# The second product of the MLP as plain matrix products in all eight batches

## The chip, the cores and the metric

The kernel runs on one core of one Trainium2 chip. The metric is the device time of one execution in microseconds, as the median of several runs. TensorE is called PE here, VectorE DVE, ScalarE ACT, GpSimd POOL and SyncE SP. SP issues nearly all transfers.

## What is computed

The inputs are q, k, v (8 batches, 8 heads, 576 tokens, 64 features), p (32 packed tokens for each batch and head) and the MLP's `w_in` (512 x 2048), `w_out` (2048 x 512) and `beta` (2048).

```python
def sm_attn(qq, kk, vv):
    s = scale * np.matmul(qq, kk.transpose(0, 1, 3, 2))
    a = np.exp(s - np.max(s, axis=-1, keepdims=True))
    return np.matmul(a / (np.sum(a, axis=-1, keepdims=True) + 1e-09), vv)
p_packed = sm_attn(p, k, v)                 # 32 tokens for each head
out = sm_attn(q, p_packed, p_packed)        # 576 tokens for each head
x = out.transpose(0, 2, 1, 3).reshape(4608, 512)
h = x @ w_in
g = h * (1.0 / (1.0 + np.exp(-beta * h)))
result = g @ w_out                          # the second product
```

## The kernel before

The work is done batch by batch, 576 tokens each: 512 "main" tokens and 64 "rest" tokens. The attention's value product is folded into the MLP's first matrix: for each batch the packed values are multiplied by `w_in` (`fused_w`, steps `w`; eight matmuls on 32-column strips of the array), and the result, scaled by the softmax sum and by beta, is `W_bf` (steps `W`, DVE). The hidden layer is then `W_bf` times the attention weights `A2T`: 16 steps `h` for a batch, each two matmuls of 512 columns into one PSUM bank, followed by SiLU on ACT (steps `g`, line 827). The 64 rest tokens are done in two steps `hr` of 16 small matmuls and two steps `gr` on ACT; the rests of two batches share one tile.

The second product, `g @ w_out`, has two forms:

- Batches named in `PLAIN` (0 and 1) use `product` in `plan_mlp`: for each block `t` of 128 tokens, 16 matmuls of 512 columns are summed in one of two output banks (eight steps `o` of two matmuls). A `take` on DVE copies the bank to SBUF; batch 0 is taken in two halves (`HALVED`), the second by an `add`.
- Batches 2 to 7 use `plan_seven`: the product is cut into 2 x 2 blocks and computed with seven block products where the plain way needs eight. Each of `P1` to `P7` is 16 matmuls of 256 columns in four quarters (keys `p` and `P`). Sums and differences of blocks of `g` are made on DVE (`S` 1 to 4, line 1013), those of blocks of `w_out` once (`T4`, line 987). Ten reads (`R`, lines 1043 and 1045) for each such batch, shared by DVE and ACT, combine the partial results.

The rest tokens of each pair of batches have a plain block of their own, `t = 4`, in both forms.

Attention of a batch, in PE's steps: `s1r` and `s1` (scores of p and k), `z1` (sums), `pun` (packed values), `s2` (scores of q), `z2` (sums). Between them ACT does the exponentials (`e1`, `e2`, `l2`, `n2`; line 397 loads an activation table at each change between exponential and SiLU) and DVE makes `A2`. In batches 0 and 1, k and q are transposed on PE (`tr`); from batch 2 on by a DMA transpose that SP issues (line 527) when the casts to bf16 on POOL (line 463) are done. `p_tr` transposes p of batches 2 to 7, after its copy `p_dup` on POOL.

The order on each engine is written out by hand: `SEQUENCE` holds one list for each engine, and each engine works through its list in order, waiting at a step until what it needs is there. `Planner.run` only merges the lists into one program; the costs given to each task serve that merge, and they set how many filler matmuls on an identity matrix (`keep_warm`) are put into gaps that the merge sees on PE in the first 60 us. SP's list is also the order of transfers: inputs of batches 0 and 1 in pieces, four 1 MB pieces each of `w_in` and `w_out` through three staging buffers, then one batch after the other. The rests of a batch are two small transfers (`ld b x 2`, line 442).

Of the kernel before, what the change touches and what calls it, by code (L numbers as in the profile page):

```python
# [8 lines left out]
B, H, S, D = 8, 8, 576, 64  # L9
# [15 lines left out]
SR = 64  # L25
# [13 lines left out]
WN = 1  # L39
# [6 lines left out]
TILED_US = 0.095  # L46
PORT = ("S", "T4", "A2", "cast", "w_in", "w_out", "p_dup", "p0_bf")
PLAIN = (0, 1)
# [7 lines left out]
        ("brow", 0), ("tr", 0, "k", 0), ("tr", 0, "k", 1), ("p0_tr", 0), ("p0_tr", 1), ("bcol",), ("brow", 1),  # L56
        ("trr", 0, "k"), ("s1r", 0), ("tr", 0, "q", 0), ("brow", 2), ("s1", 0, 1), ("s1", 0, 0), ("tr", 0, "q", 1),
        ("z1", 0), ("pun", 0, 0), ("pun", 0), ("brow", 3), ("s2", 0, 0), ("z2", 0, 0), ("z2", 0, 1), ("w", 0, 0),
        ("w", 0, 1), ("h", 0, 1), ("h", 0, 2), ("tr", 1, "k", 0), ("h", 0, 0), ("h", 0, 3), ("tr", 1, "k", 1),
        ("o", 0, 0, 1), ("o", 0, 1, 1), ("h", 0, 7), ("h", 0, 4), ("o", 0, 1, 3), ("w", 0, 2), ("trr", 1, "k"),  # L60
        ("o", 0, 0, 3), ("h", 0, 5), ("h", 0, 8), ("s1r", 1), ("trr", 0, "q"), ("h", 0, 6), ("o", 0, 1, 5),
        ("s1", 1, 0), ("o", 0, 0, 5), ("o", 0, 0, 7), ("h", 0, 11), ("s1", 1, 1), ("h", 0, 9), ("o", 0, 1, 7),
        ("o", 0, 2, 1), ("w", 0, 3), ("o", 0, 2, 3), ("o", 0, 3, 1), ("o", 0, 3, 3), ("o", 0, 2, 5), ("z1", 1),
        ("o", 0, 3, 5), ("h", 0, 14), ("o", 0, 2, 7), ("h", 0, 15), ("tr", 1, "q", 0), ("h", 0, 13), ("pun", 1, 0),
        ("h", 0, 12), ("pun", 1), ("tr", 1, "q", 1), ("h", 0, 10), ("o", 0, 3, 7), ("s2", 0, 1), ("s2", 1, 0),
        ("o", 0, 1, 9), ("o", 0, 0, 9), ("w", 1, 0), ("o", 0, 0, 11), ("o", 0, 1, 11), ("z2", 1, 0), ("o", 0, 1, 13),
        ("trr", 1, "q"), ("o", 0, 1, 15), ("z2", 1, 1), ("z2", 0, 2), ("o", 0, 0, 13), ("o", 0, 0, 15),
        ("o", 0, 3, 9), ("o", 0, 3, 11), ("s2", 1, 1), ("w", 1, 1), ("o", 0, 2, 9), ("o", 0, 3, 13), ("z2", 1, 2),
        ("o", 0, 2, 11), ("w", 1, 2), ("o", 0, 2, 13), ("h", 1, 2), ("o", 0, 2, 15), ("h", 1, 1), ("o", 0, 3, 15),
        ("h", 1, 0), ("w", 1, 3), ("h", 1, 5), ("h", 1, 3), ("p_tr", 1), ("h", 1, 4), ("o", 1, 0, 1), ("h", 1, 11),  # L70
        ("p_tr", 0), ("h", 1, 6), ("o", 1, 0, 3), ("h", 1, 8), ("o", 1, 1, 1), ("h", 1, 9), ("h", 1, 10),
        ("o", 1, 1, 3), ("hr", 0, 0), ("h", 1, 7), ("o", 1, 0, 5), ("o", 1, 1, 5), ("s1r", 2), ("hr", 0, 1),
        ("s1", 2, 1), ("o", 1, 0, 7), ("s1", 2, 0), ("h", 1, 15), ("o", 1, 0, 9), ("o", 1, 0, 11), ("o", 1, 1, 7),
        ("z1", 2), ("pun", 2, 0), ("o", 1, 1, 9), ("pun", 2), ("o", 1, 1, 11), ("h", 1, 13), ("h", 1, 12),
        ("w", 2, 0), ("w", 2, 1), ("h", 1, 14), ("o", 1, 1, 13), ("hr", 1, 0), ("o", 1, 0, 13), ("o", 1, 0, 15),
        ("hr", 1, 1), ("o", 1, 1, 15), ("s2", 2, 0), ("w", 2, 2), ("o", 1, 2, 1), ("o", 1, 2, 3), ("z2", 2, 0),
        ("o", 1, 2, 5), ("z2", 2, 1), ("o", 1, 3, 1), ("s2", 2, 1), ("o", 1, 2, 7), ("o", 1, 2, 9), ("o", 1, 3, 3),
        ("o", 1, 2, 11), ("o", 1, 2, 13), ("o", 1, 2, 15), ("o", 1, 3, 5), ("o", 1, 3, 7), ("z2", 2, 2), ("h", 2, 0),
        ("h", 2, 6), ("o", 1, 3, 9), ("s1r", 3), ("o", 1, 3, 11), ("h", 2, 1), ("s1", 3, 1), ("o", 1, 4, 1),
        ("o", 1, 3, 13), ("s1", 3, 0), ("o", 1, 4, 3), ("w", 2, 3), ("o", 1, 4, 5), ("o", 1, 4, 7), ("h", 2, 2),  # L80
        ("o", 1, 4, 9), ("o", 1, 3, 15), ("z1", 3), ("pun", 3, 0), ("h", 2, 7), ("h", 2, 3), ("pun", 3),
        ("o", 1, 4, 11), ("h", 2, 8), ("h", 2, 11), ("w", 3, 0), ("w", 3, 1), ("h", 2, 9), ("h", 2, 10),
        ("o", 1, 4, 13), ("o", 1, 4, 15), ("h", 2, 5), ("h", 2, 13), ("w", 3, 2), ("w", 3, 3), ("h", 2, 4),
        ("h", 2, 12), ("p", 2, 1, 0), ("p", 2, 1, 1), ("h", 2, 15), ("h", 2, 14), ("p", 2, 1, 2), ("P", 2, 1),
        ("hr", 2, 0), ("p", 2, 2, 0), ("hr", 2, 1), ("p", 2, 2, 1), ("p", 2, 2, 2), ("s2", 3, 0), ("s2", 3, 1),
        ("P", 2, 2), ("p", 2, 6, 0), ("p", 2, 6, 1), ("z2", 3, 0), ("p", 2, 6, 2), ("P", 2, 6), ("z2", 3, 1),
        ("z2", 3, 2), ("p", 2, 5, 0), ("p", 2, 5, 1), ("s1r", 4), ("s1", 4, 1), ("p", 2, 5, 2), ("s1", 4, 0),
        ("P", 2, 5), ("p", 2, 7, 0), ("p", 2, 7, 1), ("p", 2, 7, 2), ("P", 2, 7), ("p", 2, 3, 0), ("h", 3, 15),
        ("p", 2, 3, 1), ("z1", 4), ("h", 3, 14), ("p", 2, 3, 2), ("h", 3, 1), ("pun", 4, 0), ("h", 3, 0),
        ("p", 2, 4, 0), ("h", 3, 9), ("P", 2, 3), ("h", 3, 8), ("pun", 4), ("p", 2, 4, 1), ("h", 3, 5), ("h", 3, 2),  # L90
        ("w", 4, 0), ("w", 4, 1), ("h", 3, 3), ("h", 3, 7), ("p", 2, 4, 2), ("P", 2, 4), ("h", 3, 11), ("h", 3, 10),
        ("w", 4, 2), ("w", 4, 3), ("h", 3, 4), ("h", 3, 6), ("p", 3, 1, 0), ("p", 3, 1, 1), ("h", 3, 13),
        ("h", 3, 12), ("p", 3, 1, 2), ("P", 3, 1), ("p", 3, 2, 0), ("p", 3, 2, 1), ("hr", 3, 0), ("p", 3, 2, 2),
        ("hr", 3, 1), ("P", 3, 2), ("s2", 4, 0), ("s2", 4, 1), ("p", 3, 6, 0), ("p", 3, 6, 1), ("p", 3, 6, 2),
        ("z2", 4, 0), ("p", 3, 5, 0), ("P", 3, 6), ("z2", 4, 1), ("p", 3, 5, 1), ("p", 3, 5, 2), ("z2", 4, 2),
        ("P", 3, 5), ("s1r", 5), ("s1", 5, 0), ("s1", 5, 1), ("p", 3, 7, 0), ("p", 3, 7, 1), ("h", 4, 10),
        ("p", 3, 7, 2), ("P", 3, 7), ("z1", 5), ("pun", 5, 0), ("p", 3, 3, 0), ("p", 3, 4, 0), ("p", 3, 4, 1),
        ("h", 4, 7), ("h", 4, 2), ("p", 3, 3, 1), ("pun", 5), ("p", 3, 3, 2), ("h", 4, 14), ("h", 4, 15),
        ("p", 3, 4, 2), ("P", 3, 3), ("h", 4, 0), ("h", 4, 1), ("P", 3, 4), ("w", 5, 0), ("w", 5, 1), ("h", 4, 11),
        ("h", 4, 12), ("o", 3, 4, 1), ("o", 3, 4, 3), ("h", 4, 13), ("h", 4, 8), ("o", 3, 4, 5), ("o", 3, 4, 7),  # L100
        ("h", 4, 3), ("h", 4, 6), ("w", 5, 2), ("w", 5, 3), ("hr", 4, 0), ("h", 4, 4), ("o", 3, 4, 9),
        ("o", 3, 4, 11), ("h", 4, 9), ("h", 4, 5), ("o", 3, 4, 13), ("o", 3, 4, 15), ("s2", 5, 0), ("s2", 5, 1),
        ("p", 4, 1, 0), ("p", 4, 1, 1), ("p", 4, 1, 2), ("hr", 4, 1), ("z2", 5, 0), ("P", 4, 1), ("p", 4, 2, 0),
        ("z2", 5, 1), ("p", 4, 2, 1), ("p", 4, 2, 2), ("P", 4, 2), ("p", 4, 6, 0), ("p", 4, 6, 1), ("p", 4, 6, 2),
        ("P", 4, 6), ("p", 4, 5, 0), ("h", 5, 10), ("h", 5, 11), ("p", 4, 5, 1), ("p", 4, 5, 2), ("h", 5, 7),
        ("h", 5, 3), ("P", 4, 5), ("p", 4, 7, 0), ("p", 4, 7, 1), ("z2", 5, 2), ("s1r", 6), ("p", 4, 7, 2),
        ("s1", 6, 0), ("p", 4, 3, 0), ("s1", 6, 1), ("p", 4, 3, 1), ("P", 4, 7), ("p", 4, 3, 2), ("h", 5, 15),
        ("h", 5, 13), ("P", 4, 3), ("p", 4, 4, 0), ("p", 4, 4, 1), ("h", 5, 9), ("h", 5, 1), ("p", 4, 4, 2),
        ("z1", 6), ("h", 5, 8), ("h", 5, 0), ("pun", 6, 0), ("pun", 6), ("h", 5, 2), ("h", 5, 14), ("w", 6, 0),
        ("w", 6, 1), ("h", 5, 4), ("h", 5, 5), ("P", 4, 4), ("w", 6, 2), ("h", 5, 6), ("h", 5, 12), ("p", 5, 1, 0),  # L110
        ("p", 5, 1, 1), ("hr", 5, 0), ("hr", 5, 1), ("w", 6, 3), ("s2", 6, 0), ("p", 5, 1, 2), ("P", 5, 1),
        ("p", 5, 2, 0), ("p", 5, 2, 1), ("p", 5, 2, 2), ("P", 5, 2), ("z2", 6, 0), ("s2", 6, 1), ("p", 5, 6, 0),
        ("p", 5, 6, 1), ("p", 5, 6, 2), ("z2", 6, 1), ("P", 5, 6), ("z2", 6, 2), ("s1r", 7), ("s1", 7, 0),
        ("p", 5, 5, 0), ("p", 5, 5, 1), ("s1", 7, 1), ("p", 5, 5, 2), ("p", 5, 7, 0), ("p", 5, 7, 1), ("p", 5, 7, 2),
        ("P", 5, 5), ("h", 6, 2), ("h", 6, 12), ("P", 5, 7), ("p", 5, 3, 0), ("p", 5, 3, 1), ("h", 6, 4),
# [235 lines left out]
class Kernel:  # L351
# [153 lines left out]
    def plan_attention(self, b):  # L505
# [227 lines left out]
        def weights2(i):  # L733
# [15 lines left out]
            for i in range(2)  # L749
        ]  # L750
        s2r = self.task(
            ("s2", b, 1), "PE", (0.06, 0.15), lambda: scores2("s2r", True),
            [("pp", b), ("rq", b), s2] + oldE, rank + 5, takes="att", count=2,
        )
        e2r = [
# [588 lines left out]
```

## Time and profile before

| | |
|---|---|
| Time, median of 3 runs | 246.43 us (246.19 to 246.64) |
| The profiled execution's own time | 246.91 us |
| Its span, first to last instruction | 245.1 us |
| PE busy | 231.1 us, 94% |
| PE weight loads busy | 151.0 us, 62% |
| ACT busy | 178.8 us, 73% |
| DVE busy | 148.7 us, 61% |
| POOL busy | 58.8 us, 24% |
| Moved by DMA | 54.13 MB, 221 GB/s over the span |

The span is what the profile shows; the execution's own time is 1.81 us longer, since it also holds what lies before the first and after the last instruction. Matmuls are pipelined: a row's mean duration (380 ns for 512 columns) is longer than the distance between two starts, so durations of PE are read from starts, not from the mean.

### The profile page before, as it was taken

What the parts mean: (1) busy time and instruction counts of PE and PEld (TensorE: products, weight loads), DVE (VectorE), ACT (ScalarE), POOL (GpSimd) and SP (SyncE); (2) the same over time, 40 slices, a digit from 0 to 9 for tenths busy, and PEclk for the clock granted to TensorE, in tenths of its full rate; (3) what the DMA queues carried; (4) which work ended last, traced back from release to release, by engine and by line L of the source; (5) the groups of instructions that cost most, each with busy time, mean ns of one, the idle gap of its engine ahead of it and who ended that gap; (6) DMA issues with size and microseconds to landing.
All of it is one profiled execution on the core that took longest, in us unless ns stands there. A gap on an engine that the chain in (4) does not pass through costs nothing.

```text
span 245.1 us, 5810 instructions
## 1 busy us (share of the span) xinstructions
PE 231.1 (94%) x2429; PEld 151.0 (62%) x2429; DVE 148.7 (61%) x239; ACT 178.8 (73%) x317; POOL 58.8 (24%) x75
## 2 busy tenths in 40 slices
PE   3997779989999999999999999999999999999992
PEld 3985434633464444787578744886587557667870
DVE  6455566676907937872788376843993368813521
ACT  2486959887797897797779767988798769766210
POOL 4002313206443034207430541061305000000000
PEclk9999999999999999999999999999999999999999
DMA  6999999999989999999999999995993141004024
GB/s 195 298 332 376 305 356 312 366 256 292 199 270 143 277 301 344 183 292 285 280 176 304 325 276 187 337 228 133 195 289 75 36 171 45 1 0 174 0 77 140
DMA packets 74826, 54.13 MB, mean 221 GB/s; under 512 B 42688, under 2 KB 68304, under 8 KB 74800
## 3 DMA queue, kind: packets, MB, share of 16 engines
q1 hardware_dynamic: 74496, 53.68, 85.0%
q8 instruction: 19, 0.31, 0.5%
q10 hardware_dynamic: 304, 0.07, 0.2%
q14 instruction: 7, 0.06, 0.1%
HBM read 37.23 MB, written 9.44 MB: 190 GB/s over the span
## 4 chain that ended last, share of the span: by engine, by line
PE 73%; DMA 16%; issue 5%; POOL 3%; SPq 1%; DVE 0%; POOLq 0%
PE o_ps L382 42%; PE h_ps L382 19%; DMA kr<-in_k_dram 6%; DMA k<-in_k_dram 5%; DMA v<-in_v_dram 5%; PE hr_ps L382 3%; PE w_ps L382 3%; PE s_ps L382 2%; PE z_ps L382 2%; PE pp_ps L382 1%; POOL k_bf L463 1%; POOL p_dup L1172 1%; POOL w_in_bf L1251 1%; SPq L434 0%; PE pT_ps L387 0%
## 5 line engine op out<-in xcount | busy, mean ns | idle before, releaser
L827 ACT ACTIVATE g_main<-h_ps 128x512 bf16<-128x512 f32 x128 | 71.6, 595 | 29.7 <-PE h_ps L382 29.5
L382 PEld LDWEIGHTS <-g_main 128*128 128x128 bf16 x608 | 57.0, 98 | 27.0 <-issue 4.0
L382 PE MATMUL o_ps<-w_out_bf,g_main 128*128 128x256 bf16 (+1 forms) x416 | 72.2, 306 | 0.9 <-ACT w_out_bf L1262 0.5
L382 PE MATMUL h_ps<-A2T,W_bf 128*128 128x512 bf16 x256 | 69.8, 380 | 0.9 <-DVE A2T L736 0.6
L795 DVE SCALAR_TENSOR_TENSOR W_bf<-w_ps,rz,beta_bc 128x512 bf16<-128x512 f32 x64 | 45.1, 745 | 14.5 <-PE w_ps L382 14.4
L382 PEld LDWEIGHTS <-W_bf 128*128 128x128 bf16 x512 | 32.2, 98 | 22.7 <-issue 5.5
L397 ACT ACT_TABLE_LOAD x24 | 30.8, 1283 | 1.1 <-PEq L1328 0.7
L1043 DVE TENSOR_TENSOR o_sb<-o_ps,o_sb 128x512 f32<-128x512 f32 x18 | 12.4, 690 | 24.2 <-PE o_ps L382 21.5
L382 PE MATMUL o_ps<-w_sum,g_main 128*128 128x256 bf16 x192 | 25.9, 273 | 0.0
L382 PE MATMUL o_ps<-w_sum,g_sum 128*128 128x256 bf16 x192 | 24.8, 273 | 0.0
L463 POOL CAST v_bf<-v 128x1024 bf16<-128x1024 f32 x14 | 15.0, 1082 | 37.9 <-DMA v<-in_v_dram 29.0
L382 PEld LDWEIGHTS <-g_sum 128*128 128x128 bf16 x192 | 18.1, 98 | 4.1 <-issue 0.5
L463 POOL CAST q_bf<-q 128x1024 bf16<-128x1024 f32 x12 | 13.2, 1116 | 28.2 <-DMA q<-in_q_dram 14.9
L463 POOL CAST k_bf<-k 128x1024 bf16<-128x1024 f32 x14 | 15.2, 1101 | 16.7 <-DMA k<-in_k_dram 9.7
L382 PE MATMUL o_ps<-w_out_bf,g_rem 128*128 128x512 bf16 x64 | 16.3, 380 | 0.0
L382 PE MATMUL o_ps<-identr 128*128 128x128 bf16 x132 | 11.7, 244 | 3.7 <-DVE bones L1108 3.7
L1045 ACT COPY o_sb<-o_ps 128x512 f32<-128x512 f32 x12 | 7.0, 587 | 10.0 <-PE o_ps L382 10.0
L382 PE MATMUL w_ps<-w_in_bf,pp 64*32 64x512 bf16 x256 | 11.9, 383 | 2.3 <-POOL w_in_bf L1251 1.3
L382 PEld LDWEIGHTS <-identr 128*128 128x128 bf16 x132 | 9.5, 111 | 5.7 <-DVE bones L1108 3.7
L382 PEld LDWEIGHTS <-pp 64*32 64x32 bf16 x384 | 4.3, 89 | 13.5 <-issue 9.3
L695 ACT ACTIVATE E2T<-s_ps,rz 128x512 bf16<-128x512 f32 x16 | 10.7, 688 | 1.8 <-PE s_ps L382 1.3
L736 DVE TENSOR_TENSOR A2T<-E2T,rz 128x512 bf16<-128x512 bf16 x16 | 11.1, 691 | 1.4 <-ACT rz L731 1.4
(99 smaller groups left out, 261.1 us busy)
## 6 DMA issues: line engine op xcount, KB each, us to landing
out_dram<-o_sb SPq DMA_DIRECT2D x14, 512.0 KB, 3.6
k<-in_k_dram SPq DMA_DIRECT2D x6, 1024.0 KB, 8.9
q<-in_q_dram SPq DMA_DIRECT2D x6, 1024.0 KB, 9.1
v<-in_v_dram SPq DMA_DIRECT2D x6, 1024.0 KB, 8.1
w_in<-in_moe_w_in_dram SPq DMA_DIRECT2D x4, 1024.0 KB, 10.3
w_out<-in_moe_w_out_dram SPq DMA_DIRECT2D x4, 1024.0 KB, 10.5
k<-in_k_dram SPq DMA_DIRECT2D x4, 512.0 KB, 9.8
q<-in_q_dram SPq DMA_DIRECT2D x4, 512.0 KB, 7.6
```

The costliest lines, as they stand in the source:

```text
L382: return self.nc.tensor.matmul(out, lhsT, rhs, start=start, stop=stop, tile_position=pos, skip_group_check=True)
L397: self.nc.scalar.preload_act_table_set(SETS[mode])
L463: self.copy[engine](o[:, 0:2048].rearrange("p (t h d) -> p h t d", t=4, h=8)[:, h], t[:, 0:2048].rearrange("p (h t d) -> p h t d", h=8, t= ...
L695: nc.scalar.activation(st[b, "E2"][:, i, 0:SM], st[b, "s2", i][:], AF.Exp, scale=st[b, "rz1"][:, 2 + i : 3 + i])
L736: nc.vector.tensor_tensor(part(st[b, "A2"], i), part(st[b, "E2"], i), st[b, "rz2"][:, i] if i < 2 else st[b, "rz2r"][:], ALU.mult)
L795: nc.vector.scalar_tensor_tensor(st[b, "W"][:, r, cols], st[b, "w", m][:], st[b, "rz1"][:, r : r + 1], self.beta_bc[:, cols], op0=ALU.mult ...
L827: nc.scalar.activation(st[b, "g"][:, ft, :], st[b, "h", ft][:], AF.Silu)
L1043: nc.vector.tensor_tensor(o, x, o, ALU.add)
L1045: self.copy[engine](o, x)
L1172: self.copy[engine](self.p_dup[0:LATER, :, e, :], self.p32[0:LATER])
L1251: self.copy[engine](self.w_in_bf[:, c, 512 * n : 512 * n + 512], self.t["w_in", n][:, c])
```

## The change

`PLAIN` names all eight batches, so `plan_seven` isn't called any more, and `plan_sums` (the sums of blocks of `w_out`) is no longer called. The rest block of the last pair of batches is computed as two halves of 256 columns (`t = 4` and `t = 5`), each with its own copy and its own stores, one of each two stores issued by ACT. The lists of all five engines are replaced by others. The costs by which the lists are merged are changed a little. In the lists below only the parts are left that are spoken of later: the first transfers of SP and PE's steps about the third batch's first scores.

```diff
-TILED_US = 0.095
+TILED_US = 0.11
-PLAIN = (0, 1)
+PLAIN = tuple(range(B))
...
     "PE": [
...
-        ("o", 1, 1, 3), ("hr", 0, 0), ("h", 1, 7), ("o", 1, 0, 5), ("o", 1, 1, 5), ("s1r", 2), ("hr", 0, 1),
-        ("s1", 2, 1), ("o", 1, 0, 7), ("s1", 2, 0), ("h", 1, 15), ("o", 1, 0, 9), ("o", 1, 0, 11), ("o", 1, 1, 7),
+        ("h", 1, 4), ("h", 1, 0), ("w", 1, 3), ("o", 0, 3, 15), ("s1r", 2), ("s1", 2, 0), ("o", 1, 0, 1),
...
     "SP": [
-        ("ld", 0, "k", 0), ("ld", 0, "k", 1), ("ld", "p0", 1), ("ld", 0, "k", 2), ("ld", 0, "q", 0),
-        ("ld", 0, "v", 0), ("ld", 0, "q", 1), ("ld", 0, "v", 1), ("ld", 0, "v", 2), ("ld_in", 0), ("ld_in", 1),
-        ("ld_out", 0), ("ld", 1, "k", 0), ("ld", 1, "k", 1), ("ld_in", 2), ("ld", 1, "k", 2), ("ld", 0, "q", 2),
-        ("ld_out", 1), ("ld_in", 3), ("ld", 1, "q", 0), ("ld", 1, "v", 0), ("ld", 1, "v", 1), ("ld", 1, "v", 2),
-        ("ld", 1, "q", 1), ("ld_out", 2), ("ld_out", 3), ("ld", 1, "q", 2), ("ld", 2, "k", 0), ("ld", 2, "k", 2),
-        ("ld", "p"), ("ld", 2, "q", 0), ("ld", 2, "v", 0), ("ld", 2, "q", 2), ("ld", 2, "v", 2), ("tr", 2, "k", 0),
-        ("ld", 3, "k", 0), ("store", 0), ("ld", 3, "k", 2), ("tr", 2, "q", 0), ("tr", 3, "k", 0), ("store", 1),
+        ("ld", 0, "k", 0), ("ld", 0, "q", 0), ("ld", 0, "k", 1), ("ld", 0, "k", 2), ("ld", "p0", 1),
+        ("ld", 0, "q", 1), ("ld", 0, "v", 0), ("ld", 0, "v", 1), ("ld", 0, "v", 2), ("ld", 0, "q", 2), ("ld_in", 0),
+        ("ld_in", 1), ("ld_out", 0), ("ld", 1, "k", 0), ("ld", 1, "k", 1), ("ld", 1, "k", 2), ("ld_in", 2),
+        ("ld_in", 3), ("ld_out", 1), ("ld", 1, "v", 0), ("ld", 1, "q", 0), ("ld", 1, "v", 1), ("ld", 1, "q", 1),
+        ("ld", 1, "v", 2), ("ld", "p"), ("ld_out", 2), ("ld", 1, "q", 2), ("ld_out", 3), ("ld", 2, "k", 0),
+        ("ld", 2, "k", 2), ("ld", 2, "q", 0), ("ld", 2, "v", 0), ("ld", 2, "q", 2), ("tr", 2, "k", 0),
+        ("ld", 2, "v", 2), ("tr", 2, "q", 0), ("store", 0), ("store", 1), ("ld", 3, "k", 0), ("ld", 3, "k", 2),
...
+                n = slice(256 * (t - 4), 256 * (t - 3)) if halves and t >= 4 else slice(0, DM)
                 self.mm(
-                    st[b, "o", t][:],
+                    st[b, "o", t][:, 0 : n.stop - n.start],
                     lhsT,
-                    self.w_out_bf[:, f, :],
+                    self.w_out_bf[:, f, n],
...
+        halves = b == B - 1
...
+            if halves and t >= 4:
+                nc.vector.tensor_copy(st[b, "ob", 2][:, 0, 256 * (t - 4) : 256 * (t - 3)], st[b, "o", t][:, 0:256])
+                return
...
+                n = slice(256 * (t - 4), 256 * (t - 3)) if halves else slice(0, DM)
                 for e in range(2):
                     lo = S * (b - 1 + e) + SM
-                    nc.sync.dma_start(self.out[lo : lo + SR, :], o[64 * e : 64 * e + 64, 0])
+                    queue = nc.scalar if halves and e else nc.sync
+                    queue.dma_start(self.out[lo : lo + SR, n], o[64 * e : 64 * e + 64, 0, n])
...
-        for t in range(0 if b in PLAIN else 4, 4 + b % 2):
+        for t in range(0 if b in PLAIN else 4, 4 + b % 2 + halves):
...
         self.plan_weights()
-        self.plan_sums()
```

## The prediction, made before the result was known

> **What bounds the kernel now.** I read the page's busy times first, then a table of stretches, then the chain of waits back from the end, then the order of time around the places where PE waits.
>
> ```profile
> PE 231.1 (94%) x2429; PEld 151.0 (62%) x2429; DVE 148.7 (61%) x239; ACT 178.8 (73%) x317; POOL 58.8 (24%) x75
> PEclk9999999999999999999999999999999999999999
> ```
>
> PE is the engine without slack, at full clock throughout. The table of stretches (columns: busy of PE, PEld, DVE, ACT, POOL with instruction counts, clock, DMA share, GB/s) says where its idle time lies:
>
> ```profile
> 3.68:21.10 17.42, 15.91 (x204) 14.51 (x205) 8.55 (x27) 9.69 (x16) 1.96 (x2) 1.00 1.11 327
> 21.10:32.96 11.86, 9.02 (x98) 5.56 (x97) 7.31 (x12) 9.42 (x14) 2.93 (x3) 1.00 1.10 324
> 32.96:49.24 16.28, 15.65 (x160) 8.13 (x161) 11.50 (x21) 13.68 (x24) 3.67 (x5) 1.00 1.09 347
> 49.24:62.12 12.88, 11.92 (x88) 4.49 (x88) 9.06 (x17) 10.74 (x23) 5.30 (x6) 1.00 1.10 279
> 62.12:240.72 178.60, 178.56 (x1880) 118.34 (x1880) 109.29 (x161) 133.99 (x241) 42.03 (x51) 1.00 0.80 194
> ```
>
> From 62.12 us to 240.72 us PE is never idle; before that it waits for data, and DMA is busy without a break (share over 1 means several transfers at once). Part of the early "busy" is filler:
>
> ```profile
> L382 PE MATMUL o_ps<-identr 128*128 128x128 bf16 x132 | 11.7, 244 | 3.7 <-DVE bones L1108 3.7
> ```
>
> The end of the chain shows that the last block of PE, one copy and one store set the finish:
>
> ```profile
> 225.41 11.35 PE o_ps L382 x104
> 236.76 0.47 PE hr_ps L382 x16
> 237.22 3.47 PE o_ps L382 x16
> 240.72 0.69 DVE o_rest L892
> ```
>
> **A measure to work with.** From distances between starts in the order of time: `h` 0.4335 us, a plain piece `o` (two 512-column matmuls) 0.4325, a quarter of a block product (four of 256) 0.4365, `hr` 0.466, `w` 0.217, a change into or out of the 32-column strips 0.11, `z2` 0.216, PE transposes of 8 blocks 0.45, and so on. Summing PE's list before from `p_tr` 1, which starts at 62.12, to its end gives 178.3 us; the trace has 178.6. So these prices hold within 0.3 us, for both forms. Ahead of `p_tr` 1 the list holds 21 `h` (9.10), 32 `o` (13.84), 8 `w` (1.74), beta rows (3.80), transposes (4.44), attention of two batches (4.30), 18 changes (1.98): 39.2 us. PE reaches it at 62.12, so its **delay** (filler and waits) is 22.9 us, and the end is 217.5 us of work + 22.9 + 0.3.
>
> **What the Trainium skill says.** "TensorE: Matmul & The Clock Gate", section "Wait — 56ns, not 53.3ns?": a warm matmul takes its columns at 2.4 GHz plus about 2.5 ns, so 215.7 ns for 512 columns. The trace agrees: 16 in 3.47 us are 217 ns; eight of 256 take 0.87 us, 109 ns each, so halving the width gains nothing for a product but its own columns. "PSUM — Partial Sum Buffer", section "Engine vs sequencer instructions": matmuls start and complete in program order; so one that waits holds all behind it, as the idle stretches above show. "ScalarE: Activation LUTs", section "What ACT_TABLE_LOAD costs": 1283 ns, which is the trace's mean too (24 loads, 30.8 us), plus a drain that I cannot separate.
>
> **The change, part by part.**
>
> *Second product, batches 2 to 7.* Removed: 6 batches x 7 products x 4 quarters = 168 x 0.4365 = 73.3 us. Added: 6 x 4 blocks x 8 pieces = 192 x 0.4325 = 83.0 us. PE has no idle time there, so all of it is on the path: **+9.7 us**. The new list has 64 changes of strips for 60: +0.4. The last rest block in halves: 16 x 0.219 for 8 x 0.4325: 0. Sum of the list: 227.7 us for 217.5, **+10.2**.
>
> *DVE and ACT.* Gone: 24 sums `S` (7.3 x 4 = 29.2 us), 4 sums `T4` (4.8), 30 reads on DVE (12.4 + 8.3), 12 on ACT (7.0). New: 24 copies x 0.69 = 16.6 on DVE. DVE sheds 38 us, but PE covers all of it: it waited for neither from 62 us on, so **0**. ACT's list changes between exponential and SiLU 33 times for 23: +10 x 1.28 = 12.8 us less 7.0 for the reads. At 185 us of some 255 that too is under PE; without cover it would be up to 1.3 us for each change.
>
> *The start.* DMA is its bound, so I place arrivals by bytes. Before, the first `w_in` piece (4.6 MB in the queue up to it) is in at 19.46, the third (8.8 MB) at 31.6, `w_out`'s last (15.5 MB) at 51.6, k of batch 2 (16.6 MB) at 56.7, p at 58.7: about 0.33 MB/us, slower for small pieces. The new SP list puts the rest of q 0 (0.13 MB, two DMAs) ahead of `w_in`, the rest of k 1 ahead of its third piece, the fourth ahead of `w_out`'s second, and p (0.39 MB) ahead of `w_out`'s third and all of batch 2. First `w_in` about 0.5 us later; third near 32.8, so `w` 2 near 34.3 with 14.4 us of work done (delay 19.9; before 32.96 - 13.95 = 19.0). Against it, `h` of batch 0 starts some 0.5 us sooner, since ACT no longer casts `w_in` ahead of the logarithm. `w_out`'s last about 53.3. Each such wait leaves the delay between 22 and 24 us at 54 us.
>
> *The third batch's k.* Its DMA transpose before:
>
> ```profile
> 56.67 1.55 POOL L463 CAST k_bf<-k 128x1024 bf16<-128x1024 f32 x1 [3.91 <-DMA k<-in_k_dram]
> 61.11 5.16 SPq L527 DMA_TRANSPOSE kT<-k_bf  x1
> DMA to landing us min/median/max: 7.2/7.2/7.2
> L382 PE MATMUL s1r_ps<-pT,kT x2: 219/220/220, 68.9 to 69.0; 128*128 128x128 bf16 x2
> ```
>
> It lands at 68.3, and `s1r` 2 starts at 68.9 with 46.0 us of work ahead of it (delay 22.9): only 0.6 us to spare. In the new list only 43.0 us stand ahead of `s1r` 2 (25 `h` for 28, 32 `o` for 38, one `hr` more, four changes of strips more). With a delay of 23 PE comes there at 66. The data: p moved ahead puts k 2 some 1.2 us later (57.9); POOL no longer mixes `p_dup` into the casts (1.55 + 0.40 + 1.04), so the transpose is issued at about 60.9, with v's rest moved behind it. As much data as before lies ahead of it in the queue, so it lands at 67.2 to 68.4; I take 67.7. PE waits there with all its list behind it, ACT's `e1` of batch 2 too: delay 67.8 - 43.0 = **24.8**, 1.9 more than before. Next late is `s2` 2, on q's transpose: before issued at 69.9, landed at 78.2 beside other loads; now some 67.5, since POOL casts q ahead of v, landing near 73, when `s2` 2 is due (48.2 + 24.8). I take 0; up to 1 us.
>
> *The end.* Before: PE's end to span's end 4.4 us (240.72 to 245.1). New: the last copy has 256 columns of f32, not shown before; between 0.29 (256 columns of bf16) and 0.69 (512 of f32) I take 0.42, a gain of 0.3. One of two stores goes to ACT, idle by then, saving one issue (0.55). The store of the last main block is issued about 2.3 us before PE's end and lands 3.1 us later, still inside. Tail 3.6 us (3.3 to 4.4).
>
> *Sum.* 227.7 + 24.8 + 0.3 = 252.8, + 3.6 = 256.4 us of span. The profiled execution lay 1.81 above its span, the median 0.48 below that execution; so median = span + 1.33: **257.7 us**, +4.6%.
>
> **Rivals.**
>
> 1. *The start is as good as before* (k's transpose lands by 66): delay 22.9, span 254.5, **255.8**. For: less mixing on POOL, `h` sooner. Against: the same bytes ahead of the transpose, which had 0.6 us to spare.
> 2. *Further waits in the middle*: ten more table loads inside runs of SiLU, or q's transpose of batch 2. With 0.3 us of PE for each, a quarter of its 1.28 and my choice between 0 and all of it, 3 us more: **260.7**. For: 30 us of ACT's waits are on `h`, so it runs close behind PE; only two banks take `h`. Against: the kernel before had 23 changes and lost 0.3 us in 178.
> 3. *Not slower*: the new order takes the delay out of the start. It decides when the delay is 246.4 - 1.33 - 3.6 - 0.3 - 227.7 = 13.5 us or less, for 22.9. At that point, say **246**. Against: up to the first `w` at 21.10 only 8.5 us of work exist in the list, a delay of 12.6 that the first `w_in` sets at 19.46; less than 1 us would be left for all the rest.
> 4. *A slow start*: gates add up (k 1, v 1, q 1 in a row near 45 us): delay 27 to 28, **260.5**.
>
> That the change does not do what it says is excluded: the built list has no sums, and 256-column products only in the last block.
>
> **How the numbers follow.** 257.7 as worked 0.52; rival 1 0.25; rival 2 0.12; rival 3 0.03; rival 4 0.08. Forecast's own range 256.7 to 258.8. With rival 1 and half of 2 and 4, the 8-in-10 range is 254.9 to 260.4. About 0.2% (0.5 us) is what a measurement can tell: faster 0.02, same 0.01, slower 0.97.
>
> **What would show it.** Right: PE dense from about 68 us to its end, near 253; no 256-column `o_ps` but 32; `s1r` 2 waiting for kT near 67.8; DVE busy near 111 us, 34 table loads; 3.6 us from PE's end to the end. Wrong: idle PE after 70 us (rival 2), `s1r` 2 starting by 66.5 without a wait (rival 1), or a first `w` well before 21 us (rival 3).

## The result, and the profile after

The changed kernel takes 260.34 us (259.51 to 260.87, 4 runs), the kernel before beside it 246.53 us (246.19 to 247.53): a ratio of 1.055, 95% interval 1.0506 to 1.0594. It is slower by 13.8 us. The forecast was 257.7 us, the range 254.9 to 260.4: the time lies inside, 0.06 us from its upper edge. The profiled execution took 260.87 us with a span of 259.0; the median lies 1.34 us above this span (1.33 was assumed).

The page's busy times, and the table loads among its groups:

```profile
PE 241.5 (93%) x2158; PEld 124.4 (48%) x2158; DVE 116.8 (45%) x209; ACT 182.7 (71%) x311; POOL 60.3 (23%) x76
PEclk9999999999999999999999999999999999999999
L398 ACT ACT_TABLE_LOAD x34 | 43.6, 1283 | 1.3 <-PEq L1342 0.7
```

PE's busy time grew by the expected 10 us, DVE shed 32 us, and 34 table loads are there. In the table of stretches (columns as in the one of before) the fourth row has no counterpart in before:

```profile
20.68:34.38 13.70, 9.70 (x102) 5.68 (x103) 10.81 (x16) 7.07 (x12) 3.27 (x4) 1.00 1.07 352
34.38:53.04 18.66, 14.86 (x150) 7.09 (x151) 12.89 (x25) 14.96 (x26) 4.72 (x5) 1.00 1.08 308
53.04:67.95 14.91, 14.83 (x137) 7.00 (x137) 9.57 (x18) 10.71 (x22) 6.42 (x8) 1.00 1.15 256
67.95:80.55 12.60, 11.07 (x128) 4.98 (x129) 7.44 (x16) 12.46 (x23) 0.75 (x2) 1.00 0.98 260
80.55:255.38 174.83, 174.83 (x1425) 84.78 (x1424) 64.76 (x108) 127.45 (x213) 38.22 (x45) 1.00 0.68 174
```

The fourth row is the third batch's attention: PE is idle for 1.5 us there, and ACT is busy for 12.46 of 12.60 us. PE's list holds only 9.74 us of work between `s1r` 2 (67.95) and `h` (1, 13) (80.55), so a further 1.3 us of its busy time don't advance the list: the modelled ends of matmuls ahead of gaps, and time in which matmuls stand. The same stretch of before, from `s1r` 2 on, for comparison:

```profile
68.90:82.20 13.30, 13.30 (x178) 6.96 (x177) 7.70 (x14) 11.83 (x20) 3.73 (x6) 1.00 1.12 236
```

ACT is well loaded there too, but PE has work for every microsecond.

Where the 13.9 us of span between the two profiled executions (245.1 and 259.0) went, by the measure of the prediction, the delay (start of a step less the work ahead of it in PE's list):

| part | before | after | difference |
|---|---|---|---|
| work in PE's list | 217.5 | 227.7 | +10.2 |
| delay when `s1r` 2 starts | 22.9 | 24.9 | +2.0 |
| growth from `s1r` 2 to `h` (1, 13) | 0 | 2.86 | +2.9 |
| from there to PE's end, against the price list | +0.25 | -0.1 | -0.35 |
| PE's end to the span's end | 4.4 | 3.6 | -0.8 |

The sum is 13.9.

The steps of the prediction, in the trace. The third batch's k, its DMA transpose and who waits for it:

```profile
L528 SPq DMA_TRANSPOSE kT<-k_bf x1: 4864/4864/4864, 60.8 to 60.8; - x1
  PEld L383: 0.6, 1
DMA to landing us min/median/max: 7.1/7.1/7.1
```

It was issued at 60.8, landed at 67.9, and PE's weight load waited 0.6 us for it; counted from starts this cost PE about 0.2 us, since the matmuls before it were still running. Then the waits of PE from 66 to 82 us (us in total, times, longest):

```profile
PE w_ps L383 <- ACT rz2r L723: 0.8, 1, 0.8
PE z_ps L383 <- ACT E2T L696: 0.4, 1, 0.4
PE o_ps L383 <- DVE o_sb L903: 0.2, 1, 0.2
```

and the order of time around them (start, duration, engine; the last bracket is the idle time before it):

```profile
70.84 1.28 ACT L398 ACT_TABLE_LOAD   x1
...
73.24 1.28 ACT L398 ACT_TABLE_LOAD   x1
...
75.47 0.38 PE L383 MATMUL z_ps<-E2T,bones 128*128 128x512 bf16 x1 [0.37 <-ACT E2T L696]
...
77.17 0.64 PE L383 MATMUL w_ps<-w_in_bf,pp 64*32 64x512 bf16 x9
...
78.32 0.27 ACT L723 ACTIVATE rz2r<-z2r_ps 128x128 f32<-128x128 f32 x1
78.61 1.28 ACT L398 ACT_TABLE_LOAD   x1
78.64 0.88 PE L383 MATMUL w_ps<-w_in_bf,pp 64*32 64x512 bf16 x15 [0.83 <-ACT rz2r L723]
...
79.90 1.08 ACT L828 ACTIVATE g_main<-h_ps 128x512 bf16<-128x512 f32 x2
80.55 0.59 PE L383 MATMUL h_ps<-A2T,W_bf 128*128 128x512 bf16 x2
```

Two things meet. The new list puts the last three `w` blocks of the batch in a row behind `z2` 2, and each takes two PSUM banks of the attention's pool; the second block stops after one matmul, because ACT has not yet read the rest sums (`rz2r`, 78.32), and the third is late in its turn. And ACT, which goes from exponentials to two SiLU, back, and to SiLU again, reaches g (1, 11) only at 79.90. Until that has emptied a bank of `h`, `h` (1, 13) cannot start.

The finish, from the chain and the order of time at the end:

```profile
246.71 8.69 PE o_ps L383 x56
...
254.13 2.25 ACTq L915 DMA_DIRECT2D out_dram<-o_rest  x2
255.42 0.42 DVE L895 COPY o_rest<-o_ps 128x256 f32<-128x256 f32 x1 [1.32 <-PE o_ps L383]
```

PE ends at 255.38, the last copy takes 0.42 us, the span ends at 259.0.

### The profile page after: what moved, and what is told of

The parts are those of the page before. It is cut to its first block, busy times and chain, and to the rows that moved or that the text cites. A ratio compares the mean times of both kernels' runs of the same rounds, so it can differ in the third digit from the quotient of the medians.

```text
span 259.0 us, 5230 instructions
## 1 busy us (share of the span) xinstructions
PE 241.5 (93%) x2158; PEld 124.4 (48%) x2158; DVE 116.8 (45%) x209; ACT 182.7 (71%) x311; POOL 60.3 (23%) x76
## 4 chain that ended last, share of the span: by engine, by line
PE 76%; DMA 12%; SPq 5%; ACT 3%; DVE 2%; issue 1%; POOL 0%; DVEq 0%
PE o_ps L383 45%; PE h_ps L383 19%; DMA w_out<-in_moe_w_out_dram 5%; DMA q<-in_q_dram 4%; SPq L435 3%; PE hr_ps L383 3%; DMA k<-in_k_dram 3%; PE w_ps L383 3%; PE s_ps L383 2%; PE z_ps L383 1%; PE pp_ps L383 1%; ACT L398 1%; DVE w_out_bf L1277 1%; SPq L1260 1%; SPq L443 1%
## 5 line engine op out<-in xcount | busy, mean ns | idle before, releaser
L383 PE MATMUL o_ps<-w_out_bf,g_main 128*128 128x512 bf16 x512 | 133.0, 379 | 0.2 <-DVE o_sb L903 0.2
L383 PE MATMUL h_ps<-A2T,W_bf 128*128 128x512 bf16 x256 | 72.6, 379 | 2.6 <-DVE W_bf L796 1.2
L383 PEld LDWEIGHTS <-g_main 128*128 128x128 bf16 x512 | 46.3, 98 | 51.1 <-issue 4.3
L899 DVE COPY o_sb<-o_ps 128x512 f32<-128x512 f32 x32 | 22.0, 690 | 70.0 <-PE o_ps L383 69.9
L383 PE MATMUL o_ps<-w_out_bf,g_rem 128*128 128x512 bf16 (+1 forms) x80 | 17.8, 337 | 0.0
L383 PE MATMUL w_ps<-w_in_bf,pp 64*32 64x512 bf16 x256 | 12.7, 383 | 3.3 <-DVE w_in_bf L1266 1.2
L848 ACT ACTIVATE g_rem<-hr_ps 128x512 bf16<-128x512 f32 x16 | 9.5, 596 | 8.4 <-PE hr_ps L383 7.6
L737 DVE TENSOR_TENSOR A2T<-E2T,rz 128x512 bf16<-128x512 bf16 x16 | 13.1, 842 | 1.7 <-ACT rz L732 1.7
L383 PEld LDWEIGHTS <-pp 64*32 64x32 bf16 x384 | 4.4, 89 | 17.1 <-issue 13.8
L720 ACT ACTIVATE rz<-z_ps 128x512 f32<-128x512 f32 x16 | 9.5, 600 | 2.8 <-PE z_ps L383 2.4
L383 PEld LDWEIGHTS <-g_rem 128*128 128x128 bf16 x80 | 7.4, 98 | 6.8 <-issue 1.3
L383 PE MATMUL hr_ps<-A2T,W_bf 128*128 128x64 bf16 x256 | 10.1, 193 | 0.0
```

Of the source, the lines that this page charges most:

```text
L383: return self.nc.tensor.matmul(out, lhsT, rhs, start=start, stop=stop, tile_position=pos, skip_group_check=True)
L720: nc.scalar.activation(st[b, "rz2"][:, i], ps[:], AF.Ln)
L737: nc.vector.tensor_tensor(part(st[b, "A2"], i), part(st[b, "E2"], i), st[b, "rz2"][:, i] if i < 2 else st[b, "rz2r"][:], ALU.mult)
L848: nc.scalar.activation(st[b // 2, "gr"][:, 8 * half : 8 * half + 8, o : o + 64], st[b, "hr", half][:].rearrange("p (f n) -> p f n", f=8), ...
L899: nc.vector.tensor_copy(st[b, "ob", t // 2][:, t % 2], st[b, "o", t][:])
```

## The experiments

Chips differ by up to 0.6% in the kernel before (246.5 to 247.9 us), so ratios are taken to the kernel before on the same chip. A ratio is the one on record, with its 95% interval; the ratio of the two medians shown beside it can differ from it by up to 0.3%.

**e1. The plain product on the lists of before.** Every quarter of the seven products becomes plain pieces at the same places, and sums and reads go. The copies and stores stand where the new blocks end; nothing else of the new order.

```diff
-PLAIN = (0, 1)
+PLAIN = tuple(range(B))
...
-        self.plan_sums()
```

> The kernel before with its own lists, but batches 2 to 7 use the plain second product: each quarter of a block product on PE's list is replaced in place by plain pieces (32 for 28 in each batch), the sums and reads are gone, and 24 copies take their place on DVE. The rest block stays whole. Theory 1 (PE is the bound, the product costs 192 x 0.4325 - 168 x 0.4365 = 9.7 us and nothing covers it; what the new lists add is their own): 246.5 + 9.7 = 256.2 us, delay of PE's list still 22.9 to 23.2 us at its end. Rival (the plain product itself brings waits, on copies and on the two output banks): 258 to 260. Rival (part of the product's time is hidden after all): below 254.

Measured 257.38 us against 247.78, ratio 1.0371 (1.0309 to 1.0434): +9.2 us (the medians lie 9.6 apart). In its trace PE ends at 250.51, 9.8 us behind the 240.72 of before, with 9.7 us more in its list. PE began `p_tr` 1 1.1 us sooner than in before and lost most of this again at `s2` 2, where it waited 0.75 us; the profile names a copy on DVE, but q's transpose landed only then (78.3). So the product's form alone costs about what its count of pieces says, theory 1, and on top of it the new order loses: the changed kernel is slower still.

**e2. Seven products as before, only the last rest block in halves.**

```diff
...
-                nc.sync.dma_start(self.out[lo : lo + SR, :], o[64 * e : 64 * e + 64, 0])
+                queue = nc.scalar if halves and e else nc.sync
+                queue.dma_start(self.out[lo : lo + SR, n], o[64 * e : 64 * e + 64, 0, n])
...
```

> The kernel before with only one part of the change: the last rest block in two halves of 256 columns, each with its own copy and stores, one of two stores on ACT. PE's end stays at 240.7 us, the tail behind it falls from 4.4 to 3.6 us: 246.5 - 0.8 = 245.7 us. If the tail is set by the store's landing alone and not by copy and issue, no change (246.5).

Measured 247.42 us against 247.78, ratio 0.9963 (0.9937 to 0.999): -0.9 us by the ratio, though the medians lie only 0.4 apart, so the size is uncertain. In its trace PE ends at 240.86 and the span at 244.5, 3.7 us for 4.4. This is the one part of the change that gains, and by the ratio it is the fastest kernel of the study.

**e3. One table.** The changed kernel with an exponential in place of SiLU (SiLU is left out), so that ACT loads one table once; the rest steps `gr` are edited alike. **e4** is the same edit on the kernel before.

```diff
-            nc.scalar.activation(st[b, "g"][:, ft, :], st[b, "h", ft][:], AF.Silu)
+            nc.scalar.activation(st[b, "g"][:, ft, :], st[b, "h", ft][:], AF.Exp)
...
-                [h], rank, ends=[h], table="silu",
+                [h], rank, ends=[h], table="exp",
```

> The changed kernel with Exp in place of SiLU (SiLU's function is left out), so that ACT loads one table once instead of 34 times. Theory A (the 2.9 us that PE loses between the third batch's first scores and 81 us are lost to ACT's chain with its table loads): delay at the first scores of batch 2 still about 24.9 us, since kT lands then, and no more at the end: 257.4 us. Theory B (those 2.9 us are lost to banks and copies on DVE): 259.5 to 260.3. If kT's landing isn't what holds the first scores, the start gets faster too, the delay there falls to 22 to 23, and the time to about 255.5.

> The same in the kernel before (Exp for SiLU, one table load for 24). PE had 0.6 us to spare at the first scores of batch 2 and no wait after 62 us: 245.9 to 246.5 us by every theory in which PE and the loads of the start set the time. If ACT's table loads hold this kernel too, 244 or less.

e3 measured 258.97 us, ratio 1.0421 (1.0381 to 1.046); e4 247.86, ratio 1.000 (0.9976 to 1.0024). Table loads cost the kernel before nothing that these runs can tell (0.6 us to each side). For the changed kernel the ratio is 1.3% lower than in the result and 0.7% lower than in e5 below, the same kernel on another chip (there the intervals overlap): 1.7 to 3.2 us, which looks like theory A. Its trace doesn't bear that out in full. `h` (1, 13) starts 12.18 us after `s1r` 2, only 0.4 less than in the profile of after, and the largest wait is still there:

```profile
PE w_ps L383 <- ACT rz2r L723: 0.8, 1, 0.8
PE o_ps L383 <- DVE o_sb L903: 0.5, 1, 0.5
```

Nearly all of its shorter span (256.9 for 259.0) came from the start: `s1r` 2 ran at 65.91 for 67.95, and in e5, with all its table loads, it ran at 65.87 too (span 257.2). So e3 fits neither theory alone: with the table loads gone, the banks held PE at nearly the same place.

**e5 to e7. Two things in parallel?** e5 is the changed kernel once more. e6 spreads the `w` blocks; e7 does so and has one table (SiLU is left out, as in e3). Of the list only the pieces are shown that move.

```diff
-("z2", 2, 2), ("w", 2, 1), ("w", 2, 2), ("w", 2, 3), ("o", 1, 1, 7), ("o", 1, 1, 9), ("h", 1, 13),
+("z2", 2, 2), ("w", 2, 1), ("o", 1, 1, 7), ("o", 1, 1, 9), ("w", 2, 2), ("w", 2, 3), ("h", 1, 13),
```

> The changed kernel once more, unaltered, beside the next three on the same chip. Ratio to before 1.051 to 1.059 (about 260.3 us where before takes 246.5). The delay (start in the trace less the work ahead in PE's list) again grows by 2.9 us between s1r 2 and h(1,13); the arrivals of the first loads, and with them the delay at s1r 2, may shift by up to 1 us between executions.

> Two product pieces that come after the last w block of the third batch are put between its second and third block, so that w does not ask for six PSUM banks of attention in a row (two changes of strips more, +0.22 us). Theory 'banks': PE's 1.0 + 0.5 us at w 2 and w 3 are the cause and go, less the two changes: -1.2 us on the changed kernel. Theory 'two holds': ACT's chain of exponentials and four table loads ends in the same place, since g(1,11) comes behind it and frees the bank for h(1,13), so h(1,13) still starts 12.3 to 12.7 us after s1r 2 (12.6 in the trace of after) and the time is that of the changed kernel within 0.3 us.

> SiLU is left out (exponential in its place) so that ACT loads one table, and the w blocks are spread as in e6. Theory 'two holds': with ACT's table loads gone only the banks held PE in e3 (1.0 + 0.7 us at w), so now h(1,13) starts 11.0 to 11.3 us after s1r 2 (12.2 in e3, 9.7 of it work) and the time is 1.0 to 1.3 us below e3, a ratio to before of about 1.037. Theory 'ACT alone': no gain over e3 (1.042).

All three on one chip (the kernel before there: 247.9 us): e5 259.74 us, ratio 1.049 (1.0442 to 1.0537); e6 259.86, 1.0487 (1.0448 to 1.0527); e7 258.59, 1.0448 (1.0395 to 1.0501). The stretch, in the four traces and e3:

| | `s1r` 2 starts | `h` (1, 13) starts | between | growth of the delay |
|---|---|---|---|---|
| after | 67.95 | 80.55 | 12.60 | 2.86 |
| e5, unaltered | 65.87 | 78.70 | 12.83 | 3.10 |
| e6, `w` spread | 67.10 | 79.88 | 12.78 | 2.82 |
| e3, one table | 65.91 | 78.09 | 12.18 | 2.44 |
| e7, both | 66.89 | 77.98 | 11.09 | 1.14 |

In e6 the waits of PE from 66 to 81 us show what took the place of the banks:

```profile
PE h_ps L383 <- ACT g_main L828: 1.0, 1, 1.0
PE z_ps L383 <- ACT E2T L696: 0.4, 1, 0.4
```

The wait for `rz2r` is gone, and PE stands a microsecond at `h` (1, 13) instead (12.78 us, just above the 12.3 to 12.7 expected): no gain, as "two holds" said. With both taken away most of the loss goes, and ACT has slack; the stretches of e7:

```profile
66.89:77.98 11.09, 10.71 (x127) 4.93 (x128) 6.35 (x14) 7.84 (x18) 0.92 (x2) 1.00 0.91 243
77.98:98.79 20.81, 19.41 (x161) 9.69 (x155) 6.69 (x12) 10.59 (x20) 9.62 (x12) 1.00 1.22 239
```

So within the stretch the matter is settled: ACT's chain with its table loads and the packing of `w` each hold PE to about the same time. In the whole time e7 misses its forecast (1.0 to 1.3 us below e3, a ratio near 1.037): its ratio is 1.0448, and e3's was 1.0421. By the time alone "no gain over e3" is not refuted; only the trace speaks for two holds. Beside e5, on the same chip, e7 is 1.15 us faster, and these intervals overlap too. The second row says where the gain went: PE is idle for 1.4 us again, and its waits from 82 to 140 us are

```profile
PE s1r_ps L383 <- DMA kT<-k_bf: 0.9, 1, 0.9
PE pp_ps L383 <- POOL v_bf L474: 0.5, 1, 0.5
```

k's transpose and v's cast of the fourth batch were late next. That transpose landed 8.0 us after its issue here, and 5.8 to 6.8 in after, e5, e6 and e3, where PE didn't wait for it. From the start of `s1r` 2 to its end PE takes 187.9 us in e7 and 187.4 to 187.8 in the other four (the lists of e6 and e7 hold 0.2 us more): in this trace all that was gained in the stretch was lost again. The execution took 260.21 us, 1.6 above e7's median, so it need not be so in all of them. That the kernel would be 2.9 us faster without the two holds is therefore not shown; what is shown is where PE loses them.

**e8 and e10. Is it k's transpose that sets `s1r` 2?** e8 puts 1.3 us of work ahead of the second batch's last q transposes, where PE waits 1.8 us for data; e10 adds that DVE casts half of the third batch's k, so that its transpose is issued sooner (the move of this cast from POOL's list to DVE's is not shown).

```diff
-("pun", 1, 0), ("tr", 1, "q", 1), ("h", 0, 9), ("h", 0, 15), ("pun", 1), ("o", 0, 3, 1), ("o", 0, 2, 5),
+("pun", 1, 0), ("h", 0, 9), ("h", 0, 15), ("o", 0, 2, 5), ("tr", 1, "q", 1), ("pun", 1), ("o", 0, 3, 1),
...
+                late = "DVE" if (b, x) == (2, "k") else "POOL"
-                self.task(("cast", b, x, 1), "POOL", 0.97, lambda f=piece: f("POOL", 1, 4), [m0, c0], rank + 3)
+                self.task(("cast", b, x, 1), late, 0.97, lambda f=piece, e=late: f(e, 1, 4), [m0, c0], rank + 3)
```

> Two h and one product piece (1.3 us of PE's work) are put ahead of the second batch's last q transposes, where PE waited 1.8 us for q's load. Theory 'kT' (the step of the prediction): s1r 2 is set by the DMA transpose of k 2, so it starts where it did (67.7 to 68.0, or 7.1 us after the transpose's issue) and the PE's wait for kT there grows from 0.6 to 1 or more; time as the changed kernel within 0.3 us. Theory 'early gates' (q's load alone sets the delay): the gain is kept, s1r 2 starts 0.7 to 1.3 us sooner, and the time falls by as much.

> As e8, and the second half of k's cast in the third batch goes to VectorE (0.69 us, beside the first on GpSimd) in place of GpSimd, so that k's DMA transpose is issued about 0.6 us sooner after k has landed. Theory 'kT': with 1.3 us of work ahead of q's transposes, kT was what held s1r 2 in e8 (PE waited 0.5 us for it); now that wait is gone or under 0.1 us, and the delay at s1r 2 is that of trr 1 q at 53 us, no more than 0.1 above it. Theory 'early gates': the same delay as in e8, since kT is not what holds it. In the time the two differ by at most 0.5 us, which the medians cannot tell; the trace decides. The 2.8 to 3.1 us that PE loses between s1r 2 and h(1,13) stay.

e8: 259.46 us, ratio 1.0469 (1.0424 to 1.0515), 0.3 us under e5 on the same chip, as "kT" said; but its trace is not clean evidence. At the transposes of q's rest (`trr` 1, q; near 53 us) its delay was 23.33, against 22.87 in e5, so the filled step's gain was gone before k mattered, and PE's wait for kT was 0.5 us, not 1 or more. In e5 the transposed k was in before PE came, and PE didn't wait at all. e10: 260.56 us against 246.68, ratio 1.0561 (1.0542 to 1.0581), and a miss for both theories, with a delay at `s1r` 2 some 0.6 us above that at `trr` 1, q:

```profile
L530 SPq DMA_TRANSPOSE kT<-k_bf x1: 5491/5491/5491, 60.1 to 60.1; - x1
  DMA kT<-k_bf: 1.4, 2
DMA to landing us min/median/max: 7.7/7.7/7.7
```

The transpose was issued only 1.9 us after the first cast of k began (2.4 in after) but took 7.7 us for 6.6 to 7.1, and the wait stayed. From the start of that cast to the landing there are 9.0 us (e5), 9.3 (e8), 9.5 (after) and 9.6 (e10): in e10 the earlier issue brought no earlier landing. What holds it in the queues was not separated. So the early gates and kT lie within a microsecond of each other, and none of these runs moves the one without the other.

**e9. The parts without the new order: e1 and e2 together.**

> The plain product in all batches on the lists of before (as e1) together with the last rest block in halves (as e2): the two useful or needed parts of the change without its new order. If the parts add up: +9.2 us (e1) - 0.9 us (e2) = +8.3 us, a ratio to before of 1.034, that is 3.5 to 5 us under the changed kernel measured before it. If the new order helped the product somewhere, the time would be at or above e1's 1.037.

Measured 256.97 us against 246.68, ratio 1.0412 (1.0389 to 1.0435): +10.3, where the parts added to 8.3. That is above e1's 1.037, which was to mean that the new order helps; but neither e1 nor e9 has the new order, so it can't mean that. Its trace has PE without a gap from `p_tr` 1 to its end:

```profile
62.83:251.49 188.66, 188.61 (x1608) 91.97 (x1608) 74.90 (x127) 128.20 (x229) 41.29 (x51) 1.00 0.74 183
```

The list holds 9.75 us more work than before, the tail is 3.6 us; the rest of its span (255.1 for 245.1) is a delay of 23.63 for 22.92 at `p_tr` 1 and 0.35 more growth from there on, most of it at `h` (3, 4). In e1 the delay at `p_tr` 1 was 21.86, with the same order. So the plain form is worth 9.2 to 10.3 us by the two timings and 9.75 by the list, and the spread is in the start, whose part in the medians stays open. Against e9, the changed kernel's new order costs another 0.8% (e5) to 1.4% (the result) of the time before, 2 to 3.4 us; e10, on e9's chip and with two small edits, lies 1.5% above it. In the two profiled executions PE ends 3.9 us later than in e9 (255.38 and 251.49): 0.4 of it is a longer list, 1.3 the delay at `s1r` 2, and 2.1 what PE loses from there on.

## Why the prediction was right or wrong

- **The time:** the range holds it, but in part by luck. It reaches to 260.4 because it took in half of the rivals 2 and 4; the forecast's own range of 256.7 to 258.8 was missed by 1.5 us. The sign named for rival 2, idle PE after 70 us, was there.
- **The product, +9.7 us, and the list, +10.2:** right. PE's list sums to 227.7 us and its end agrees with it within 0.4; e1 measures the product at 9.2 us, and e9, with a tail that gains, at 10.3; at PE's end e1's trace has 9.8.
- **The start.** `w` 2 predicted near 34.3, measured 34.38. "Each such wait leaves the delay between 22 and 24 us at 54 us" was too low for this execution: it was 24.7 at 53.04, with 1.8 us at q's load of the second batch, 0.8 at the first `z2` behind a table load, 0.6 at q's rest. It was right for e5 (22.9) and e6 (24.0).
- **k's transpose, delay 24.8:** the number was met (24.92, `s1r` 2 at 67.95 for 67.8, transpose issued at 60.8 for 60.9), but its reading as the one cause was not. In this execution the waits before it had used up 24.7 of it; in e5 kT was in time and the delay was 22.84. PE stands behind whichever of two gates is later, as in the rivals 1 and 4, and which one it is changes between executions. Rival 4's 260.5 us came near by luck: the delay was 24.9, not 27 to 28.
- **`s2` 2, 0 us:** right. q's transpose was issued at 67.21 and landed 5.3 us later; `s2` 2 started at 73.73 without a wait for it.
- **"ACT ... too is under PE: so 0" for the ten further table loads:** this is the step that failed. The cover was judged by ACT's total (185 us of 255; it came to 182.7). In the stretch behind `s1r` 2 ACT had no slack, and PE lost 2.86 and 3.10 us in the two traces of the kernel, and 2.82 in e6, where ACT alone holds it. Nor is it the table loads alone: e3, without them, still loses 2.44, and only e7, without both, gets to 1.14. The packing of `w`, on which the prediction has no word, is the second hold. How much of this the whole time would win back stays open, since e7's PE lost as much again at the fourth batch. A drain beside a load, which the prediction could not separate, does not show: at the first change of the stretch SiLU ends at 67.68, the load runs from 67.70 to 68.98, and the next step starts at 69.00.
- **Rival 2** gave 260.7 us for "further waits in the middle" and named both ACT's closeness to PE and the two banks of `h`. Its size was right, its place was not: not 0.3 us at each of ten changes, but all of it in one stretch of 12.6 us.
- **The end, 3.6 us, with 0.42 us for the copy:** right to the digit, and e2's trace shows it by itself (3.7).
- **DVE, 111 us:** 116.8, under PE all the same; what the other 5.8 us are was not looked into.

The sum: 257.7 + 2.9 for the stretch + 0.1 for the start - 0.4 for the rest of the list is 260.3, which is the median measured. The terms are those of one execution; in e5 the start was 2 us better and the stretch 0.2 worse.

## What to carry to other kernels

"Hidden under the busy engine" is a statement on a place, not on a total: take each stretch between two steps that depend on the other engine, and compare what that engine must do there in order with the work that the busy engine's list holds for it; here 12.5 us stood against 9.7, while the totals were 183 against 242. When a wait is taken away and nothing is gained, look for a second one that ends at the same time before the first is called harmless, and test both together; then follow the busy engine to its end, since the next late transfer can take the gain back, as in e7. And a reordering that a change brings with it should be timed apart from the change: here e9 and e1 show that most of the loss is the plain form's longer work on PE, and that the order made it worse.

## What was not expected of the hardware

- The start of one and the same kernel moves between executions by more than the effects searched for: `w` 2 starts at 34.38 in one and at 33.14 in another, `s1r` 2 at 67.95 and 65.87, counted from the span's first instruction, with times of 260.87 and 258.99 us.
- In e10 a cast on DVE and one on GpSimd ran side by side, and both were long: DVE's 0.87 us where the same form takes 0.69 elsewhere, GpSimd's 0.86 us for a rest of 256 columns that took 0.40 in the changed kernel. That kernel has such a cast too, in the fourth batch, while DVE makes `A2T` (1.34 us):

```profile
81.82 0.86 POOL L474 CAST k_bf<-kr 128x256 bf16<-128x256 f32 x1
```

  What lengthens them was not tested.
- The landing of one and the same DMA transpose moves: 6.6 to 7.7 us after its issue for the third batch's k in seven traces of the changed kernel and its variants, 5.8 to 8.0 for the fourth's in five of them.
